# Gate logits by transposes and a VectorE sum instead of a product with a 0/1 matrix

## The chip, the cores and the metric

The kernel runs on one core of one Trainium2 chip. The metric is the device time of a run in microseconds (us); the median of three runs of the kernel before is 718.48 us (718.31 to 719.34). Engines are named as in the profile: PE is TensorE (PEld its weight loads), DVE is VectorE, ACT is ScalarE, POOL is GpSimd, SP is SyncE, which here only issues transfers.

## The reference

A linear attention with decay over 4 batches, 8 heads, 768 positions and 64 channels gives a matrix `x` of 3072 tokens by 512 columns. A mixture of 8 experts follows, in which every token goes to its two best experts. The change concerns the lines that compute `logits` and the argument of `noise_scale`, which are two products of `x` with 512 x 8 matrices.

```python
out[:, :, sl] = intra + inter                       # attention, block by block
kv_state = lam_block * kv_state + einsum('bhsd,bhse->bhde', kb_dec, vb)
...
x = attn_out.transpose(0, 2, 1, 3).reshape(B * S, H * D)     # 3072 x 512
...
logits = x @ w_gate                                 # 512 x 8
noise_scale = np.log1p(np.exp(x @ w_noise))         # 512 x 8
noisy_logits = logits + noise_scale * noise
top2 = np.argpartition(-noisy_logits, 2, axis=1)[:, :2]
...                                                 # softmax weights of the two
h = np.maximum(x[mask] @ w1[e], 0.0)
out[mask] += top2_w[mask, k, None] * (h @ w2[e])
```

## The kernel before

The attention handles 256 positions of all heads at once, as two chunks of 128, which is one unit `u` of 12. A loop over `t` from 0 to 11 (below: step 0 to step 11) is software-pipelined by hand: the order of the code is the order on every engine, since the schedule is manual. In step `t` the kernel does, in this order:

- `products(t-1)` and `turn_x(t-1)`: from the attention output `xo` of the unit before, four matmuls with the gate weights `wgn` (each leaves 32 rows of the PSUM tile `pR`, one for each of the four 128-column blocks of `x`, of which 16 are gate and noise products), copied by ACT into `xp` (128 rows x 2 chunks x 128 tokens); and eight transposes of `xo` into `xc`, which is stored to DRAM.
- `trans_k(t+1)`, `trans_q(t+1)`, `kv(t+1)`: transposes of keys and queries, scaling of the queries on DVE (`qTs`), and the decayed state `S`, which POOL multiplies and DVE adds to.
- `intra(t)`, `inter(t, 0)`, `evac_o(t)`: the output matmuls into `pO` and `pKV`.
- `logits(t-1)`: the rows of `xp` hold, for a token, four partial sums of each of 16 values, at rows 0, 32, 64 and 96 plus the value's number. Two matmuls (one for each chunk), with `xp` as the weights and the constant 0/1 matrix `sel` (128 x 16) as the moving operand, add the four and put tokens on the partitions, in the PSUM tile `pL`.
- `scores(t+1)`: 16 matmuls into four PSUM banks, which DVE multiplies with the decay mask into `at` (four instructions). The banks of `scores` are the ones that the transposes of the next step take, in the same order.

The PSUM tiles named `pS` rotate over four banks. `pL` is one bank; it holds the logits of a block in its first half and, in the second half, the counts and lists of the routing.

The routing works on blocks of 8 chunks (`GB`): block 0 is the chunks of units 0 to 3, and is worked on from step 4 on; block 1 from step 8 on; block 2 when the attention is over. It is a Python generator, `routing(b)`, that is drawn forward by `advance(n)` at three places of a step: in `kv` (by 4, `FILLC`), before `scores` (by 2, `FILLB`) and after them (by 18 to 24, `FILLA`). Each `yield` of the generator is one unit of `n`, mostly one small DVE instruction; `yield "step"` ends the `advance` that meets it, so that what follows begins at the next place. `gate(b)` begins with a copy of the block's logits from PSUM to `l2`. Then come `zc`, `ga`, an exponential (`gn` to `ge`), a logarithm (`glacc`), the noisy logits `nl`, the maxima `mx` and `mi`, the one-hot `oh` and `ob`; `weights(b)` (`wa` to `ws`, `recs`); `count(b)`, matmuls of `ob` on PE into `pL`; and `route(b)`: `own`, two large comparisons into a `wst` buffer (called `hot` in the code, five units each), `pos`, `past`, `rest`, then `yield "step"`, then 24 small matmuls (`tokab`) into `pL` with `hot` and `rest` as weights, and `whole`, `idx`, `found` and more on DVE.

POOL has, in steps 4 to 7, one `split_low` each (a subtraction over 128 x 1024 into `w1l`), which follows a one-element copy (`spacer`) that waits for `at`; in step 7 two gathers of token rows follow it, then the split of step 8 and the product for `S`.

After the loop, expert 0 begins on PE while DVE works on block 2. The setup of `sel` is seven DVE instructions in the prologue.

Of the kernel before, what the change touches and what calls it, by code (L numbers as in the profile page):

```python
# [21 lines left out]
FT = mybir.dt.float32  # L22
FR = mybir.dt.float32r
BF = mybir.dt.bfloat16
I32 = mybir.dt.int32
U32 = mybir.dt.uint32
AF = mybir.ActivationFunctionType
OP = mybir.AluOpType
AX = mybir.AxisListType

B, H, S, D = 4, 8, 768, 64
C = 128
# [4 lines left out]
DB = DM // 128  # L37
E = 8
# [32 lines left out]
GB = (0, 8, 16, NCH)  # L71
NG = len(GB) - 1
GM = max(GB[i + 1] - GB[i] for i in range(NG))
# [46 lines left out]
def kernel(  # L120
# [3 lines left out]
    nc = tc.nc  # L124
    MULT, ADD, SUB = OP.mult, OP.add, OP.subtract

    dram = ctx.enter_context(tc.tile_pool(name="dram", bufs=1, space=bass.MemoryType.DRAM))
    consts = ctx.enter_context(tc.tile_pool(name="consts", bufs=1))
    psum = ctx.enter_context(tc.tile_pool(name="psum", bufs=1, space=bass.MemoryType.PSUM))
    wp = ctx.enter_context(tc.tile_pool(name="wp", bufs=1, side="right"))  # L130
    rp = ctx.enter_context(tc.tile_pool(name="rp", bufs=1, side="right"))
    att = ExitStack()
    ac = att.enter_context(tc.tile_pool(name="ac", bufs=1))
    aw = att.enter_context(tc.tile_pool(name="aw", bufs=2))
# [39 lines left out]
    keep_warm(WARM[0])  # L174
    for nm in ("kt", "qt"):
        load(0, nm)
    jp = ac.tile([128, 128], I32, name="jp")
    nc.gpsimd.iota(jp, pattern=[[1, 128]], base=0, channel_multiplier=-1)
    identf = consts.tile([128, 128], FT, name="identf")
    nc.vector.tensor_scalar(identf, jp, 0.0, None, op0=OP.is_equal)  # L180
# [12 lines left out]
    p = psum.tile([128, H], FT, name="pL")  # L193
# [13 lines left out]
    p = psum.tile([128, HP, C], FT, name="pL")  # L207
# [1 line left out]
        nc.tensor.matmul(p[:, hp, :], hsel[:, hp].rearrange("h s i -> h (s i)"), pw[:, 127::-1], start=True, stop=True)  # L209
    nc.scalar.activation(QS, p, AF.Copy)  # L210
    nc.scalar.dma_start(mrev.rearrange("p i h -> p (i h)"), sub(powd, 0, [[H, 128], [1, C * H]]))

    sel = consts.tile([128, 2 * E], FT, name="sel")
    sq4 = ac.tile([128, 2 * E], FT, name="sq4")
    nc.vector.tensor_scalar(sel, jp[:, 0:2 * E], 0.0, None, op0=OP.is_equal)
    for d in range(1, DB):
        nc.vector.tensor_scalar(sq4, jp[:, 0:2 * E], float(-32 * d), None, op0=OP.is_equal)
        nc.vector.tensor_add(sel, sel, sq4)

    for nm in ("kt", "qt", "vt"):  # L220
        load(1, nm)
# [53 lines left out]
    jobs, scatters, PL = [], [], {}  # L275
# [23 lines left out]
    qT, qTs, kT, KD, AT, XO, XP, PO, SA, first = {}, {}, {}, {}, {}, {}, {}, {}, {}, {}  # L299

    pl, PC = None, {}
# [137 lines left out]

    def logits(u):  # L440
        nonlocal pl
        for a in range(2):
            g = 2 * u + a
            b = max(i for i in range(NG) if GB[i] <= g)
            if not g:
                pl = psum.tile([128, 512], FT, name="pL")
            if g == GB[b]:
                PL[b] = pl[:, b % 2 * 128:][:, :GM * 2 * E].rearrange("p (c e) -> p c e", e=2 * E)
                PC[b] = pl[:, 256 + b % 2 * 128:]
            nc.tensor.matmul(PL[b][:, g - GB[b], :], XP[u][:, a, :], sel, start=True, stop=True)  # L450


    def gate(b):
        v = nc.vector
        gs = GB[b + 1] - GB[b]
        sh = [128, gs, E]
        t = lambda sh, nm, dt=FT: rp.tile(sh, dt, name=nm)
        pl = PL[b]
        l2 = t([128, gs, 16], "l2")
        v.tensor_copy(l2, pl[:, :gs, :])  # L460
        yield
        zc = t(sh, "zc")
        v.tensor_scalar(zc, l2[:, :, 8:16], 87.0, -87.0, op0=OP.min, op1=OP.max)
        yield
        z = zc.rearrange("p c e -> p (c e)")
        fl = [128, gs * E]
        a = t(fl, "ga")
        v.scalar_tensor_tensor(a, z, -1.0, z, op0=MULT, op1=OP.max)
        yield
        e = t(fl, "ge")  # L470
        yield from exp_neg(nc, rp, e, a, fl, "g")
        acc = t(fl, "glacc")
        v.tensor_scalar(acc, e, LOGC[-1], None, op0=MULT)
        yield
        for c in LOGC[-2::-1]:
            v.scalar_tensor_tensor(acc, acc, c, e, op0=ADD, op1=MULT)
            yield
        acc3 = acc.rearrange("p (c e) -> p c e", e=E)
        v.scalar_tensor_tensor(acc3, l2[:, :, 8:16], 0.0, acc3, op0=OP.max, op1=ADD)
        yield  # L480
        nl = t(sh, "nl")
        v.tensor_mul(nl, acc.rearrange("p (c e) -> p c e", e=E), nz[:, GB[b]:GB[b + 1], :])
        yield
        v.tensor_add(nl, nl, l2[:, :, 0:8])
        yield
        mx = t(sh, "mx")
        mi = t(sh, "mi", U32)
        for c in range(gs):
            v.max(mx[:, c, :], nl[:, c, :])
            yield  # L490
        for c in range(gs):
            v.max_index(mi[:, c, :], mx[:, c, :], nl[:, c, :])
            yield
        ei = t([128, 2, gs], "ei")
        v.tensor_copy(ei.rearrange("p r c -> p c r"), mi[:, :, 0:2])
        yield
        oh = t([128, 2, gs, E], "oh")
        v.tensor_tensor(oh, iota8[:, :, :gs, :], ei[:, :, :, None].to_broadcast([128, 2, gs, E]), op=OP.is_equal)
        yield
        ob = t(sh, "ob", BF)  # L500
        v.tensor_add(ob, oh[:, 0], oh[:, 1])
        yield
        RT[b] = dict(mx=mx, ei=ei, oh=oh, ob=ob)
# [476 lines left out]
    for t in range(NST):  # L980
        u = t + 1
# [267 lines left out]
    with tc.For_i(0, n_over) as it:  # L1249
# [16 lines left out]
        for f in range(FB):  # L1266
            p = psum.tile([128, OV], FT, name="pS", bufs=4)
# [7 lines left out]
        p = psum.tile([OV, DM], FT, name="pO")  # L1275
# [35 lines left out]
```

## Time and profile before

| | |
|---|---|
| median of three runs | 718.48 us |
| the profiled execution, its own time | 711.21 us |
| its span, first to last instruction | 709.3 us |
| PE busy | 692.0 us (98%) |
| DVE, ACT, POOL busy | 358.1, 241.4, 287.3 us |
| granted TensorE clock, mean | 0.999 of full speed |
| `logits`, PE line L450 | 48 records for 24 matmuls, from 34.1 to 137.9 us |

The span is the profiled execution; about 1.9 us lie around it. Matmuls of 32-bit data show two records for each instruction, transposes one. A timeline row gives a start, the time from the start of the first to the end of the last of the instructions that it merges, the engine, the code line, the operation, the tiles (out<-in), the shape, the count and, in brackets, the idle time of the engine ahead of it with what ended it. A row of the chain of work gives a start, the time that the chain spent there, the engine, the tile and the line. A step of the attention takes about 10 us, and `pL L450` in a row marks its `logits`.

### The profile page before, as it was taken

How to read it: one execution, taken by the hardware profiler on the slowest of the kernel's cores; microseconds unless marked ns; L12 is line 12 of the kernel's file. 1: busy time of each engine (PE TensorE's matmuls, PEld its weight loads, DVE VectorE, ACT ScalarE, POOL GpSimd, SP SyncE). 2: the span in 40 equal slices, each digit the busy share in tenths (PEclk: the TensorE clock that was granted, in tenths of full speed). 3: DMA queues.
4: the chain of work that ended last, by engine and by line, in shares of the span. 5: the costliest groups of instructions: out<-in, count | busy, mean ns of one | idle time of the engine just before them, and what ended most of it. 6: DMA issues, size and time to landing. Idle time of an engine off the chain costs nothing.

```text
span 709.3 us, 13691 instructions
## 1 busy us (share of the span) xinstructions
PE 692.0 (98%) x5005; PEld 602.1 (85%) x5005; DVE 358.1 (50%) x817; ACT 241.4 (34%) x457; POOL 287.3 (41%) x447
## 2 busy tenths in 40 slices
PE   8899999899999999999999999999999999999996
PEld 6788888699898898889888988898988898889885
DVE  6345879787236565453635263635553454345211
ACT  1667785432133441231333133313422232304200
POOL 6211455677853547622144214424431524221311
PEclk9999999999999999999999999999999999999999
DMA  9999998582525668764377537756665646530211
GB/s 204 212 241 248 250 244 248 190 262 80 119 64 173 189 189 229 164 197 149 124 250 227 171 116 246 230 168 229 214 185 165 219 151 189 171 124 28 67 46 39
DMA packets 142731, 124.34 MB, mean 175 GB/s; under 512 B 88108, under 2 KB 110764, under 8 KB 142661
## 3 DMA queue, kind: packets, MB, share of 16 engines
q1 hardware_dynamic: 127844, 84.04, 44.2%
q0 software_dynamic: 14400, 38.87, 18.2%
q8 instruction: 40, 0.66, 0.4%
q10 hardware_dynamic: 416, 0.53, 0.2%
q14 instruction: 31, 0.25, 0.1%
HBM read 87.21 MB, written 37.32 MB: 176 GB/s over the span
## 4 chain that ended last, share of the span: by engine, by line
PE 75%; DVE 6%; DMA 6%; issue 6%; SPq 4%; ACT 1%; POOL 1%; POOLq 0%; DVEq 0%; ACTq 0%
PE pS L863 33%; PE pKV L906 12%; PE pO L906 12%; PE pS L932 4%; DMA turned<-ot 3%; PE pS L358 2%; PE pKV L371 2%; SPq L156 2%; PE pO L371 2%; SPq L842 1%; PE pS L431 1%; DMA crossed<-ot 1%; DVE at L361 1%; PE pS L315 1%; PE pS L328 1%
## 5 line engine op out<-in xcount | busy, mean ns | idle before, releaser
L863 PE MATMUL pS<-xth,w1h 128*128 128x512 f32 (+3 forms) x544 | 181.3, 333 | 2.0 <-DVE ht L873 1.6
L863 PE MATMUL pS<-xtl,w1h 128*128 128x512 f32 (+3 forms) x544 | 180.8, 332 | 0.5 <-DVE xtl L828 0.5
L863 PE MATMUL pS<-xth,w1l 128*128 128x512 f32 (+3 forms) x544 | 180.6, 332 | 0.0
L869 ACT ACTIVATE ht<-pS 128x512 fp32r<-128x512 f32 (+3 forms) x136 | 65.3, 482 | 220.8 <-PE pS L863 214.6
L873 DVE SCALAR_TENSOR_TENSOR ht<-pS,ht 128x256 fp32r<-128x256 f32 (+3 forms) x152 | 74.4, 501 | 104.8 <-ACT ht L869 102.8
L863 PEld LDWEIGHTS pS<-xth,w1h 128*128 128x128 f32 x544 | 102.8, 189 | 11.6 <-DVE ht L873 2.1
L863 PEld LDWEIGHTS pS<-xtl,w1h 128*128 128x128 f32 x544 | 102.8, 189 | 9.5 <-DVE xtl L828 0.6
L863 PEld LDWEIGHTS pS<-xth,w1l 128*128 128x128 f32 x544 | 102.8, 189 | 8.7
L906 PE MATMUL pKV<-w2h,ht 128*128 128x512 f32 x336 | 108.0, 393 | 0.0
L906 PE MATMUL pO<-w2h,ht 128*128 128x512 f32 x336 | 107.7, 392 | 0.0
L816 POOL DMA_INDIRECT xg<-x_tok,rec x46 | 52.7, 1145 | 90.4 <-DVE xtl L850 44.3
L906 PEld LDWEIGHTS pKV<-w2h,ht 128*128 128x128 f32 x336 | 63.2, 188 | 13.9
L906 PEld LDWEIGHTS pO<-w2h,ht 128*128 128x128 f32 x336 | 63.2, 188 | 13.7
L906 PE MATMUL pO<-w2l,ht 128*128 128x512 f32 x168 | 65.8, 391 | 0.0
L906 PE MATMUL pKV<-w2l,ht 128*128 128x512 f32 x168 | 65.8, 391 | 0.0
L960 POOL DMA_INDIRECT out_dram<-pv,rec x28 | 40.2, 1436 | 37.3 <-DVE pv L955 21.8
L625 POOL DMA_INDIRECT lst<-recs,dest x48 | 48.5, 1011 | 11.0 <-issue 8.3
L890 POOL DMA_INDIRECT pv<-out_dram,rec x39 | 40.0, 1027 | 28.5 <-issue 21.6
L960 POOL DMA_INDIRECT out_dram<-ot,rec x18 | 23.2, 1288 | 66.6 <-DVE ot L918 61.7
L849 ACT ACTIVATE xth<-xg 128x512 fp32r<-128x512 f32 (+1 forms) x39 | 22.7, 598 | 74.9 <-DMA xg<-turned 74.9
L1209 POOL COPY spacer<-ht 1x1 f32<-1x1 f32 x53 | 9.4, 177 | 88.0 <-ACT ht L869 87.9
L778 DVE TENSOR_TENSOR w2l<-wst,w2h 128x1024 fp32r<-128x1024 f32 (+1 forms) x33 | 38.1, 1155 | 9.4 <-ACT w2h L774 9.4
(240 smaller groups left out, 1030.0 us busy)
## 6 DMA issues: line engine op xcount, KB each, us to landing
wst<-in_moe_w_dram SPq DMA_DIRECT2D x48, 512.0 KB, 5.9
turned<-ot SPq DMA_DIRECT2D x36, 256.0 KB, 2.9
xg<-turned SPq DMA_DIRECT2D x144, 64.0 KB, 2.0
wst<-in_moe_w_dram SPq DMA_DIRECT2D x32, 256.0 KB, 4.1
kt<-in_k_dram SPq DMA_DIRECT2D x24, 256.0 KB, 5.9
qt<-in_q_dram SPq DMA_DIRECT2D x24, 256.0 KB, 6.7
vt<-in_v_dram SPq DMA_DIRECT2D x24, 256.0 KB, 5.6
x_tok<-xc POOLq DMA_DIRECT2D x8, 512.0 KB, 5.8
```

What stands on the lines that cost most here:

```text
L371: nc.tensor.matmul(PO[u][a][half(g), hp, :], lhs, rhs, start=n == 1, stop=n == (8 if u % NW or a else 4))
L625: st = nc.gpsimd.indirect_dma_start(out=lst, out_offset=bass.IndirectOffsetOnAxis(ap=r["dest"][:, i, c:c + 1], axis=0), in_=r["rec"][:, c, ...
L778: low.tensor_tensor(lo, st, hi.bitcast(FT), op=SUB)
L816: nc.gpsimd.indirect_dma_start(out=XG[t][:size(e, t)], out_offset=None, in_=x_tok[:rows, :], in_offset=bass.IndirectOffsetOnAxis(ap=at, ax ...
L849: nc.scalar.activation(hi, p, AF.Copy)
L863: nc.tensor.matmul(p, W1[a][d][:, fs], xt(b, cs)[:, d], start=(d == 0 and i == 0), stop=(d == DB - 1 and i == 2))
L869: nc.scalar.activation(ht(e, 0, f, cs), p, AF.Relu)
L873: nc.vector.scalar_tensor_tensor(ht(e, 1, f, c), p[:, r], 0.0, ht(e, 0, f, c).bitcast(FT), op0=OP.max, op1=SUB)
L890: nc.gpsimd.indirect_dma_start(out=PV[t][:size(e, t), :], out_offset=None, in_=out, in_offset=bass.IndirectOffsetOnAxis(ap=REC[e, t][:, 0: ...
L906: nc.tensor.matmul(p, ht(e, a, f, cs), W2[b][f // 2][:, f % 2, :], start=(i == 0), stop=(i == len(terms) - 1))
L932: nc.tensor.matmul(p, W2[b][f // 2][:, f % 2, d * 128:(d + 1) * 128], ht(e, a, f, cs), start=(i == 0), stop=(i == len(terms) - 1))
L960: st = nc.gpsimd.indirect_dma_start(out=out, out_offset=bass.IndirectOffsetOnAxis(ap=REC[e, t][:, 0:1], axis=0), in_=o, in_offset=None, bo ...
```

## The change

The two matmuls with `sel` become two transposes of `xp` with the identity `identf`, and one DVE reduction adds the four blocks, out of PSUM and into `l2` in SBUF, which is now allocated when a block's first logits come. So `gate` no longer begins with a copy, and its generator has one `yield` fewer. `sel` and its setup go. The integer matrix `jp` of the prologue takes a buffer of the tile `xc`.

```diff
-    jp = ac.tile([128, 128], I32, name="jp")
+    jp = aw.tile([128, 2, DB, C], FT, name="xc")[:, 0, 0, :].bitcast(I32)
...
-    sel = consts.tile([128, 2 * E], FT, name="sel")
-    sq4 = ac.tile([128, 2 * E], FT, name="sq4")
-    nc.vector.tensor_scalar(sel, jp[:, 0:2 * E], 0.0, None, op0=OP.is_equal)
-    for d in range(1, DB):
-        nc.vector.tensor_scalar(sq4, jp[:, 0:2 * E], float(-32 * d), None, op0=OP.is_equal)
-        nc.vector.tensor_add(sel, sel, sq4)
...
     def logits(u):
         nonlocal pl
+        g = 2 * u
+        b = max(i for i in range(NG) if GB[i] <= g)
+        if not g:
+            pl = psum.tile([128, 512], FT, name="pL")
+        if g == GB[b]:
+            PL[b] = (ac if b % 2 else rp).tile([128, GM, 2 * E], FT, name="l2")
+            PC[b] = pl[:, 256 + b % 2 * 128:]
+        p = pl[:, :2 * C].rearrange("p (a x) -> p a x", a=2)
         for a in range(2):
-            g = 2 * u + a
-            b = max(i for i in range(NG) if GB[i] <= g)
-            if not g:
-                pl = psum.tile([128, 512], FT, name="pL")
-            if g == GB[b]:
-                PL[b] = pl[:, b % 2 * 128:][:, :GM * 2 * E].rearrange("p (c e) -> p c e", e=2 * E)
-                PC[b] = pl[:, 256 + b % 2 * 128:]
-            nc.tensor.matmul(PL[b][:, g - GB[b], :], XP[u][:, a, :], sel, start=True, stop=True)
+            nc.tensor.transpose(p[:, a, :], XP[u][:, a, :], identf)
+        nc.vector.tensor_reduce(PL[b][:, g - GB[b]:g - GB[b] + 2, :],
+                                p.rearrange("p a (d e) -> p a e d", d=DB)[:, :, :2 * E, :], axis=AX.X, op=ADD)
...
     def gate(b):
-        pl = PL[b]
-        l2 = t([128, gs, 16], "l2")
-        v.tensor_copy(l2, pl[:, :gs, :])
-        yield
+        l2 = PL[b][:, :gs, :]
```

The generator is drawn by the same numbers, so each of its instructions now stands one place earlier. At most places that moves one small instruction across the four `at` of a step. In step 7 it moves more. On PE there, these are the rows of the program before from `logits` on (L450 is `logits`, L358 `scores`, L371 `inter`, L586 the small matmuls of `route(0)`).

```order
L450 MATMUL pL<-sel,xp 128x16 x2
L358 MATMUL pS<-qT,kT 128x128 x16
L371 MATMUL pKV<-qTs,S_171 64x128
L371 MATMUL pO<-qTs,S_170 64x128
L371 MATMUL pKV<-qTs,S_171 64x128
L371 MATMUL pO<-qTs,S_170 64x128
L371 MATMUL pKV<-qTs,S_171 64x128
L371 MATMUL pO<-qTs,S_170 64x128
L371 MATMUL pKV<-qTs,S_171 64x128
L371 MATMUL pO<-qTs,S_170 64x128
L586 LDWEIGHTS wst
L586 MATMUL pL<-tokab,wst 128x2
```

In the changed program (lines are 7 or 8 lower: L444 is the transposes, L578 the small matmuls) the same place of PE reads as follows.

```order
L364 MATMUL pKV<-qTs,S_160 64x128
L444 MATMUL pL<-identf,xp 128x128 x2
L578 LDWEIGHTS wst
L578 MATMUL pL<-tokab,wst 128x2
L578 LDWEIGHTS wst
```

And the end of the small matmuls in the changed program, on PE, with what follows them (L351 is `scores`).

```order
L578 LDWEIGHTS rest
L578 MATMUL pL<-tokab,rest 64x2
L351 MATMUL pS<-qT,kT 128x128 x16
L364 MATMUL pKV<-qTs,S_162 64x128
L364 MATMUL pO<-qTs,S_161 64x128
```

The 24 small matmuls of step 7 stood behind `scores` and `inter` and now stand ahead of them; since they write `pL`, the first of them also waits for the DVE reduction that reads `pL`. On DVE, before, step 7 from the query scaling on (L335 is `qTs`, L411 the state sum, L361 `at`):

```order
L335 TENSOR_TENSOR qTs<-pS,QS 128x4x128 x2
L411 TENSOR_TENSOR S_171<-S_171,pS 128x256
L571 SCALAR_TENSOR_TENSOR own<-ob,pos 128x8
L575 SCALAR_TENSOR_TENSOR rest<-own,last 128x512
L361 TENSOR_TENSOR at<-pS,Mk_130 128x512
L361 TENSOR_TENSOR at<-pS,Mk_131 128x512
L361 TENSOR_TENSOR at<-pS,Mk_130 128x512
L361 TENSOR_TENSOR at<-pS,Mk_131 128x512
L589 TENSOR_REDUCE whole<-pL 128x2
L591 CAST idx_186<-whole 128x2
L593 TENSOR_REDUCE found_190<-pL 64x1
```

The same stretch of DVE in the changed program (L445 is the new reduction, L354 `at`):

```order
L563 SCALAR_TENSOR_TENSOR own<-ob,pos 128x8
L328 TENSOR_TENSOR qTs<-pS,QS 128x4x128 x2
L404 TENSOR_TENSOR S_162<-S_162,pS 128x256
L567 SCALAR_TENSOR_TENSOR rest<-own,last 128x512
L445 TENSOR_REDUCE l_1240<-pL 128x32
L581 TENSOR_REDUCE whole<-pL 128x2
L583 CAST idx_177<-whole 128x2
L354 TENSOR_TENSOR at<-pS,Mk_130 128x512
L354 TENSOR_TENSOR at<-pS,Mk_131 128x512
L354 TENSOR_TENSOR at<-pS,Mk_130 128x512
L354 TENSOR_TENSOR at<-pS,Mk_131 128x512
L585 TENSOR_REDUCE found_181<-pL 64x1
```

`own` went ahead of `qTs`; the reduction, `whole` and `idx` now stand between `rest` and `at`. In step 10 the two large comparisons of block 1 stood together on DVE; in the changed program the reduction stands between them:

```order
L543 SCALAR_TENSOR_TENSOR own<-ob,pL 128x8
L547 SCALAR_TENSOR_TENSOR wst<-own,row 128x1024
L445 TENSOR_REDUCE l_2008<-pL 128x32
L547 SCALAR_TENSOR_TENSOR wst<-own,row 128x1024
L354 TENSOR_TENSOR at<-pS,Mk_130 128x512
```

The reduction there follows the transposes of the same step, which PE reaches behind `inter`. On ACT, POOL and SP no instruction moved.

## Rows read from the trace of the kernel before

**Rows 1.** The chain of work that ended last, steps 7 to 11.

```profile
94.05 0.55 PE pL L450 x4
...
97.18 0.83 PE pL L586 x24
...
106.47 2.46 DVE at L361 x4
...
122.63 0.23 DVE ob L501
...
125.95 0.55 PE pL L450 x4
...
131.85 0.59 PE pL L450 x4
```

**Rows 2.** Busy time by stretch: us, then PE, PEld, DVE, ACT, POOL.

```profile
core 0: us, PE busy (x) PEld busy (x) DVE busy (x) ACT busy (x) POOL busy (x), PEclk, DMA share, GB/s
...
84.00:94.00 10.00, 10.00 (x169) 8.69 (x165) 9.52 (x24) 7.34 (x18) 5.09 (x6) 1.00 1.12 261
...
114.00:124.00 10.00, 9.25 (x138) 7.64 (x138) 9.76 (x44) 5.45 (x12) 6.33 (x14) 1.00 0.99 293
```

**Rows 3.** Timeline of PE, step 4 (`logits`, `scores`) and step 5 (`turn_x`, `trans_k`).

```profile
64.29 0.62 PE L450 MATMUL pL<-sel,xp 128*128 128x16 f32 x4
64.84 2.06 PE L358 MATMUL pS<-qT,kT 64*128 64x128 f32 x32
...
67.99 1.09 PE L431 MATMUL pS<-identf,xo 128*128 128x128 f32 x8
68.92 1.04 PE L315 MATMUL pS<-identf,kt 128*128 128x128 f32 x8
```

**Rows 4.** Timeline of DVE: the two reductions nearest in size, and a large product out of PSUM.

```profile
98.12 0.15 DVE L589 TENSOR_REDUCE whole<-pL 128x2 f32<-128x4 f32 x1
...
99.37 0.29 DVE L606 TENSOR_REDUCE pp<-oh 128x16 f32<-128x128 f32 x1
...
102.28 0.69 DVE L335 TENSOR_TENSOR qTs<-pS,QS 128x512 f32<-128x512 f32 x1 [2.08 <-ACT qT L331]
```

**Rows 5.** Timeline of DVE, steps 5 to 7.

```profile
76.45 2.47 DVE L361 TENSOR_TENSOR at<-pS,Mk 128x512 f32<-128x512 f32 x4
...
85.80 2.48 DVE L361 TENSOR_TENSOR at<-pS,Mk 128x512 f32<-128x512 f32 x4 [0.20 <-PE pS L358]
88.20 0.98 DVE L521 TENSOR_SCALAR ws<-we 128x8 f32<-128x8 f32 x1
...
92.96 1.28 DVE L335 TENSOR_TENSOR qTs<-pS,QS 128x512 f32<-128x512 f32 x2
...
94.68 0.69 DVE L575 SCALAR_TENSOR_TENSOR rest<-own,last 128x512 bf16<-128x512 f32 x1
95.72 2.48 DVE L361 TENSOR_TENSOR at<-pS,Mk 128x512 f32<-128x512 f32 x4 [0.35 <-PE pS L358]
```

**Rows 6.** Timeline of POOL: the splits of steps 6 and 7, the state product of step 8.

```profile
86.77 2.38 POOL L778 TENSOR_TENSOR w1l<-wst,w1h 128x1024 fp32r<-128x1024 f32 x1
...
96.69 2.36 POOL L778 TENSOR_TENSOR w1l<-wst,w1h 128x1024 fp32r<-128x1024 f32 x1
...
104.19 0.62 POOL L410 TENSOR_TENSOR S<-S,QS 128x256 f32<-128x256 f32 x1
```

**Rows 7.** Timeline of DVE, step 8, and the two comparisons of step 10.

```profile
104.84 0.42 DVE L411 TENSOR_TENSOR S<-S,pR 128x256 f32<-128x256 f32 x1 [1.54 <-POOL S L410]
105.36 0.29 DVE L460 COPY l<-pL 128x128 f32<-128x128 f32 x1
...
106.44 2.48 DVE L361 TENSOR_TENSOR at<-pS,Mk 128x512 f32<-128x512 f32 x4 [0.56 <-PE pS L358]
...
124.49 2.36 DVE L555 SCALAR_TENSOR_TENSOR wst<-own,row 128x1024 bf16<-128x1024 f32 x2
```

**Rows 8.** Waits of PE from 134 to 240 us: total, times, longest.

```profile
PE pL L535 <- DVE ob L501: 0.2, 1, 0.2
```

## The prediction

> **What bounds the kernel now.** I read the busy shares first, then the chain of work that ended last, then the timelines of PE, DVE and POOL around the rows that the change touches. The shares say PE (98%), but `logits` occurs only in the attention, so that stage has to be read by itself. There the chain of work runs along PE from step 1 to step 8, and `logits` lies on it with 0.55 us each time, as in step 7 [rows 1]. From 106.47 us on it changes to DVE: through `at` of step 8 and the gate of block 1 as far as `ob` at 122.63. PE then waits for `ob`; the rest of the way is mixed: `logits` of step 10 (125.95), `at`, the routing, `logits` of step 11 (131.85), expert 0. The busy times agree: from 84 to 94 us PE is full and DVE has 0.48 us left; from 114 to 124 us DVE is full and PE is not [rows 2]. So PE time is worth something up to step 8 only if DVE, which has almost nothing to spare from step 5 on, can follow. After 160 us PE is the bound and any shift passes through unchanged.
>
> **What goes, and its price.** *PE.* `logits` takes 64.84 - 64.29 = 0.55 us to the next group's start [rows 3]. Eight transposes of the same kind (32-bit, 128 x 128, the same identity) take 68.92 - 67.99 = 0.93 us [rows 3], so two take 0.23. The saving is 0.32 us a step; its bounds are 0 (the transposes take the old slot of 0.55 after all) and 0.32. *DVE.* The reduction reads 128 elements a partition out of PSUM and writes 32. The nearest rows are the sum over 128 elements (0.29 us) and the sum over 4 (0.15) on one side, and a product of 512 elements out of PSUM (0.69) on the other [rows 4]. I take 0.27 from one start to the next, as the 0.29 row is the nearest; the bounds are 0.15 and 0.69. There are twelve of them. Three copies of 0.29 go [rows 7], and so do seven setup instructions in the prologue: these are hidden by DVE's idle time ahead of the first key copy, which waits for PE and its first keys, and I count nothing for them.
>
> [...]
>
> **Steps 1 to 6.** In steps 1 to 4 DVE waits for PE, and the reduction fits in that wait: it needs the transposes alone, while `at` needs the first half of `scores`, which comes 95.72 - 94.60 = 1.12 us after `scores` begin (94.05 + 0.55 = 94.60 [rows 1], [rows 5]). So `at` of step 4 begins 4 x 0.32 = 1.3 us earlier. In step 5 `at` followed its predecessor on DVE with no idle time (76.45), in step 6 with 0.20 [rows 5]. There DVE sets the pace: two reductions cost 0.54. PE meets this in step 6, where its transposes want the banks that `at` of step 5 frees: I count a stall of 0.2 us. PE then comes to `logits` of step 7 6 x 0.32 - 0.2 = 1.7 us early, at 92.35, and is done with it at 92.6.
>
> **Step 7.** Here the moved order decides. The 24 small matmuls now stand ahead of `scores`, and the first of them waits for the reduction, which stands behind `rest` on DVE. When is `rest` done? Before, at 95.72 - 0.35 = 95.37 [rows 5]. Now: minus 1.3 (step 4), plus 0.54 (two reductions), minus the 0.20 that was idle, minus some 0.45 because the list stands one place further ahead. That last term is worth more than one small instruction: `ws` took 0.98 us, and ended at 89.18, when POOL's split, begun at 86.77, ended (89.15) [rows 5, 6]; it now goes ahead of `at`, and only what follows the split's end counts. The sum is -1.4: `rest` ends at 94.0, the reduction at 94.25. PE has waited 1.65 us for it, nearly all that it had gained. The small matmuls take 0.83 [rows 1]; `scores` begin at 95.08 instead of 94.60, and `at` at 96.2 instead of 95.72. Since the 0.83 no longer follows `inter`, what comes after on PE is 0.83 - 0.48 = 0.35 us earlier than before. If the split delays nothing, `rest` ends 0.7 earlier, and so does all this.
>
> **Step 8.** PE would let `at` begin 0.35 + 0.32 = 0.67 earlier. But POOL's split of step 7 waits for `at` of step 7 (+0.48); two gathers, the next split and the state product follow it in POOL's order, the last at 104.19 [rows 6], and DVE's state sum, before at 104.84 after a wait of 1.54 for that product [rows 7], waits for it. It moves to 105.32. Behind it come the reduction in the place of the copy, `zc`, and now `ga` too: before, the copy and `zc` were done at 106.44 - 0.56 = 105.88 [rows 7]; now 105.88 + 0.48, less 0.02, and `ga` makes 106.5 or a little less. `at` of step 8 begins where it was (106.44), at best 0.7 earlier. So the gain of PE's eight `logits` has gone almost entirely: to DVE, to the moved small matmuls, and to POOL behind them.
>
> **Steps 9 to 11 and expert 0.** From `at` of step 8 to `ob` DVE does the same work, with one more reduction (0.27) and one small instruction less on either side: about 0. In step 10 the reduction stands between two comparisons of 2.36 / 2 = 1.18 us each and waits for PE's transposes: the first comparison ends at 125.67 [rows 7], the transposes begin at 125.95 [rows 1] and give their result at about 126.25. DVE idles 0.6, and `at` begins at 126.5 + 1.18 = 127.7; before it was 126.50 + 1.12 = 127.62. So +0.1, and the saving of that `logits` is lost too. In step 11 `logits` is on the chain of work, after a wait for DVE: -0.3 remains. In expert 0 block 2 has no copy any more, and PE's one wait of 0.2 us for its `ob` [rows 8] goes: -0.2.
>
> The sum is 0 + 0.1 - 0.3 - 0.2 = -0.4 with the split's hold as I read it, and -1.1 without. I take -0.7, nearer to the first. The profiled execution (711.21, of which the span is 709.3) would become 710.5. It is 7.3 us below the median of the runs; the difference carries over, and the prediction is 718.48 - 0.7 = 717.8 us.
>
> **The rivals.** *The saving goes through.* PE keeps 0.32 in eight steps, and the two last terms: -2.6 - 0.5 = -3.1, 715.4. For it: `logits` is on the chain eight times in a row. Against it: `rest` was done only 0.35 us before `at` had to begin, and POOL's wait in step 8.
>
> *The reduction is dear, and the kernel slower.* At 0.69 it costs 0.42 more each time. It counts in six steps: 5 and 6 (ahead of `rest`), 7 (ahead of the small matmuls), 8, 9 and 10. That is 6 x 0.42 = 2.5, less 0.7: +1.8, 720.3. It decides from 0.12 more on, a reduction of about 0.4 us, and is measurable from 0.63. For it: the reduction's operand is read with a stride, which no row here does out of PSUM. Against it: 0.29 for as many elements with a stride of one.
>
> *The transposes save nothing*, because weight loads or the start of a group set the 0.55: then PE gains nothing, the small matmuls of step 7 come when `rest` is done at 95.4 or later, and POOL's chain moves with them: +0.5 to +1, about 719.2. Against it: the same transposes cost 0.116 each in their groups.
>
> **How the numbers follow.** Below about 0.2% (1.4 us) a difference can't be told from none here. Chances: the likeliest, 0.62, with a range of its own of 717.0 to 718.4; the saving goes through, 0.18; the dear reduction, 0.13; no saving, 0.07. Faster by over 0.2% (below 717.04) takes in the second and a tenth of the first: 0.24. Slower (above 719.92) is two thirds of the third and a little of the last: 0.10. The same: 0.66. The range is 716.0 to 719.8: it leaves out most of the second case and half of the third.
>
> **What would show it.** Right: two transposes in about 0.23 us on PE; reductions of about 0.29; in step 7 PE idle by over 1 us ahead of the small matmuls, with DVE's reduction as releaser; `at` of step 8 behind a wait for POOL; in step 10 an idle DVE ahead of the reduction. Wrong: if `scores` of step 7 begin before 94 us the stall is smaller than I make it, most of the 2.6 us is kept, and the time is near 715.5; if reductions take 0.5 or more, the kernel is slower. A change outside the attention (tiles of the later stage laid out anew, other waits there) is not in the sum at all.

## The result, and the profile after

The changed kernel is slower: 727.12 us (median of 6 runs, 724.50 to 728.49) against 717.86 us of the kernel before (6 runs beside it), a ratio of 1.0131 with an interval of 1.0111 to 1.0150. The prediction was 717.8 us, no change. Its profiled execution took 727.13 us, of which the span is 725.3, at a mean granted clock of 0.986.

Inside the attention the trace shows the new instructions much as they were priced. First the groups of the two new lines (duration min, median, max in ns; first and last start).

```profile
L444 PE MATMUL pL<-identf,xp x24: 272/314/421, 34.9 to 142.2; 128*128 128x128 f32 x24
```

```profile
L445 DVE TENSOR_REDUCE l<-pL x12: 281/289/293, 35.4 to 143.5; 128x32 f32<-128x128 f32 x12
its engine sat idle before it (us, times) until:
  PE pL L444: 4.8, 6
who waited for it (us, times):
  PE pL L578: 1.3, 1
```

PE waited for a reduction once, 1.3 us. That is step 7, in the timeline of PE:

```profile
93.84 0.44 PE L444 MATMUL pL<-identf,xp 128*128 128x128 f32 x2
95.55 0.54 PE L578 MATMUL pL<-tokab,wst 128*128 128x2 bf16 x16 [1.28 <-DVE l L445]
96.02 0.41 PE L578 MATMUL pL<-tokab,rest 128*64 128x2 bf16 x8
96.36 3.21 PE L351 MATMUL pS<-qT,kT 64*128 64x128 f32 x32
```

PE sits idle for 1.28 us ahead of the small matmuls, as forecast in kind (1.65). What was not forecast is the last row: `scores` takes 3.21 us, where the same matmuls took 2.06 in step 4 of before [rows 3]. The table of stretches says why: the column in front of the last two is the granted clock.

```profile
core 0: us, PE busy (x) PEld busy (x) DVE busy (x) ACT busy (x) POOL busy (x), PEclk, DMA share, GB/s
...
84.00:94.00 10.00, 10.00 (x167) 8.51 (x164) 9.69 (x27) 7.39 (x18) 5.16 (x6) 1.00 1.14 269
...
97.00:100.00 3.00, 3.00 (x36) 2.78 (x36) 1.69 (x3) 1.37 (x3) 1.27 (x2) 0.50 1.10 225
...
114.00:124.00 10.00, 9.94 (x150) 7.95 (x147) 9.55 (x48) 6.52 (x17) 4.19 (x10) 1.00 0.54 154
...
134.00:144.00 10.00, 6.29 (x71) 4.64 (x72) 5.70 (x26) 2.66 (x5) 6.41 (x16) 0.87 0.98 298
144.00:154.00 10.00, 10.00 (x86) 9.92 (x86) 2.54 (x9) 3.38 (x8) 2.65 (x5) 0.79 0.51 176
```

From 97 to 100 us, behind the idle stretch, the granted clock was 0.50. From 84 to 94 us PE is full as before; from 114 to 124 us PE is now full (9.94) and DVE is not (9.55), where before it was the other way round [rows 2]. `at` of step 8 came 2.42 us late (the last row here against 106.44 in [rows 7]). Not all of that is from step 7: `scores` of step 1 had begun 0.64 us late (35.29 against 34.65), behind an earlier stretch at a low granted clock (0.50 from 22 to 24 us).

```profile
107.10 0.42 DVE L404 TENSOR_TENSOR S<-S,pR 128x256 f32<-128x256 f32 x1 [0.73 <-POOL S L403]
107.78 0.29 DVE L445 TENSOR_REDUCE l<-pL 128x32 f32<-128x128 f32 x1 [0.26 <-PE pL L444]
...
108.86 1.29 DVE L354 TENSOR_TENSOR at<-pS,Mk 128x512 f32<-128x512 f32 x2 [0.30 <-PE pS L351]
```

The larger loss lies behind the attention, where the diff changes no line. The chain of work there, then the timeline of ACT:

```profile
148.19 0.61 ACT xc L425
148.81 2.91 DMA x_tok<-xc
151.82 0.39 ACT ht L861
```

```profile
139.07 0.60 ACT L384 ACTIVATE xo<-pO 128x512 f32<-128x512 f32 x1 [5.46 <-remote]
...
148.19 0.60 ACT L425 ACTIVATE xc<-pS 128x512 f32<-128x512 f32 x1 [0.37 <-PE pS L424]
151.82 0.66 ACT L861 ACTIVATE ht<-pS 128x256 fp32r<-128x256 f32 x2 [3.04 <-DMA x_tok<-xc]
```

In the kernel before, `ht` followed `xc` at once:

```profile
141.48 1.09 ACT L432 ACTIVATE xc<-pS 128x512 f32<-128x512 f32 x2 [2.95 <-PE pS L431]
142.45 0.39 ACT L869 ACTIVATE ht<-pS 128x256 fp32r<-128x256 f32 x1
```

Expert 0's first `ht` now waits for the store of the last unit's `xc` to DRAM, which it has nothing to do with. ACT's 5.46 us ahead of `xo` are of this execution alone: in the second profile of the same kernel (group 2) ACT waits 3.82 us there, for PE, as before (3.69), and the wait of `ht` is there again:

```profile
148.63 0.66 ACT L861 ACTIVATE ht<-pS 128x256 fp32r<-128x256 f32 x2 [4.69 <-DMA x_tok<-xc]
```

The program's allocation tells what ties the two: in the kernel before `ht` has bytes 22176 to 75424 of each partition and the two `xc` buffers lie from 98368 on; in the changed kernel `ht` begins at 22112, and `xc` lies at 52160 to 60352, inside it. The diff does that: `jp` is now taken out of the first `xc` tile, so that `xc` is placed early in its pool, and the dropped `sel` (64 bytes a partition) let everything behind it slide.

### The profile page after: what moved, and what is told of

Its sections match the earlier page's. It is cut to its first block, busy times and chain, and to the rows that moved or that the text cites. A ratio compares the mean times of both kernels' runs of the same rounds, so it can differ in the third digit from the quotient of the medians.

```text
span 725.3 us, 13649 instructions
## 1 busy us (share of the span) xinstructions
PE 699.7 (96%) x4981; PEld 602.2 (83%) x4981; DVE 358.6 (49%) x819; ACT 241.9 (33%) x457; POOL 287.8 (40%) x447
## 4 chain that ended last, share of the span: by engine, by line
PE 77%; DVE 8%; issue 6%; DMA 3%; SPq 2%; POOL 2%; another core or an unknown queue 1%; ACT 1%; POOLq 0%; ACTq 0%
PE pS L855 35%; PE pKV L898 13%; PE pO L898 12%; PE pS L924 5%; PE pS L351 2%; SPq L156 2%; DVE at L354 2%; PE pKV L364 2%; PE pO L364 1%; PE pS L817 1%; PE pS L424 1%; DMA vt<-in_v_dram 1%; POOL out_dram L952 1%; DVE glacc L468 1%
## 5 line engine op out<-in xcount | busy, mean ns | idle before, releaser
L898 PE MATMUL pKV<-w2h,ht 128*128 128x512 f32 x336 | 109.7, 398 | 0.0
L808 POOL DMA_INDIRECT xg<-x_tok,rec x46 | 50.8, 1104 | 84.2 <-DMA rec<-lst 33.4
L952 POOL DMA_INDIRECT out_dram<-pv,rec x28 | 42.3, 1512 | 37.9 <-DVE pv L947 20.7
```

Source lines behind the costliest of these rows:

```text
L808: nc.gpsimd.indirect_dma_start(out=XG[t][:size(e, t)], out_offset=None, in_=x_tok[:rows, :], in_offset=bass.IndirectOffsetOnAxis(ap=at, ax ...
L898: nc.tensor.matmul(p, ht(e, a, f, cs), W2[b][f // 2][:, f % 2, :], start=(i == 0), stop=(i == len(terms) - 1))
L952: st = nc.gpsimd.indirect_dma_start(out=out, out_offset=bass.IndirectOffsetOnAxis(ap=REC[e, t][:, 0:1], axis=0), in_=o, in_offset=None, bo ...
```

## The experiments

All ratios are to the kernel before in the same group of runs. The groups ran on several chips, on which the kernel before took from 709.9 to 717.6 us, so times in us are not compared across groups, and the first four expectations, written in us against 717.9 and 727.1, are to be read as ratios (720 to 722 is 1.003 to 1.006, 722 to 725 is 1.006 to 1.010, 724 to 725 is 1.0085 to 1.010, 717 to 718.5 is 0.999 to 1.001).

**Group 1: undoing the side effects.** The first run moves `jp` out of `xc`:

```diff
-    jp = aw.tile([128, 2, DB, C], FT, name="xc")[:, 0, 0, :].bitcast(I32)
+    jp = wp.tile([128, F], FT, name="wst", bufs=4)[:, :128].bitcast(I32)
```

> The changed kernel, with the index matrix jp in a tile of the weight staging ring instead of in the first xc tile, so that xc lies behind qTs and xp again as in the kernel before, and no longer under the ht tile of expert 0. Theory of the layout: expert 0's first ht no longer waits for the last store of x_tok (151.82 us in the changed kernel, 142.45 before); it begins near 145, and the time falls from 727.1 by 5 to 7 us to 720 to 722, with the 2.4 us of step 7 left. Rival (the transposes and the reduction cost the time themselves, by DVE time or by a lower clock of TensorE): the first ht is late anyway and the time stays within 1.5 us of 727.

The second makes the opposite edit alone in the kernel before:

```diff
-    jp = ac.tile([128, 128], I32, name="jp")
+    jp = aw.tile([128, 2, DB, C], FT, name="xc")[:, 0, 0, :].bitcast(I32)
```

> The kernel before, with one edit: jp in the first xc tile, so that xc comes to lie under the ht tile of expert 0. The products with the 0/1 matrix and the order of the work are as before. Theory of the layout: the first ht of expert 0 waits for the last store of x_tok and begins some 5 us late (near 148 instead of 142.45); the time is 722 to 725 instead of 717.9. Rival (transposes and reduction): no change, 717 to 719.

The third restores the order, by one `yield` in the changed kernel; the fourth has this and the edit of the first.

```diff
         l2 = PL[b][:, :gs, :]
+        yield
```

> The changed kernel with one more yield at the start of the gate, so that the routing of a block advances as it did before, and the 24 small matmuls of step 7 stand behind scores again. Layout as in the changed kernel. Theory of the moved order: no idle PE ahead of the small matmuls of step 7, no stretch at a granted clock of 0.50 in 97 to 100 us, at of step 8 near 106 instead of 108.88; the time falls by 2 to 3 us to 724 to 725, if the wait of the first ht doesn't take it back (it hangs on the last store of x, which moves along). Rival (the idle stretch comes from the reduction itself, or from the transposes): time and step 7 stay as they are, 727.

> The changed kernel with jp in the staging ring and with the additional yield: only the transposes and the reductions in place of the products are left of the change. If layout and moved order are the whole loss, 717 to 718.5, the time of the kernel before within 0.2%. If the transposes and the reduction cost time themselves, 720 or more. If their saving goes through, 715 to 716.5.

Measured: layout undone 1.0052 (1.0033 to 1.0070), layout alone 1.0045 (1.0028 to 1.0061), order undone 1.0076 (1.0057 to 1.0096), both undone 1.0029 (1.0018 to 1.0040). The first is as expected, the second and the third are somewhat lower. The two answers on the place of `xc` agree: 0.45% alone, and 0.76 - 0.29 = 0.47% between the third and the fourth. The timeline of ACT in the run with the layout alone has the wait, with products, `sel` and order as before:

```profile
141.31 1.09 ACT L432 ACTIVATE xc<-pS 128x512 f32<-128x512 f32 x2 [2.94 <-PE pS L431]
147.14 0.66 ACT L869 ACTIVATE ht<-pS 128x256 fp32r<-128x256 f32 x2 [4.75 <-DMA x_tok<-xc]
```

The price of the moved order is 0.52 - 0.29 = 0.23% here. But the fourth run doesn't fit: with both undone 0.29% is left, although its trace was 1 us ahead of before at `scores` of step 7 (93.38 us against 94.53, by the timelines). Something later took 3 us.

**Group 2: the rest.** The changed kernel again; the rest with `jp` in the free `l2` tile and the order undone; and two single edits in the kernel before (`jp` in the staging ring; no `yield` behind the gate's copy).

```diff
+    jp = ac.tile([128, GM, 2 * E], FT, name="l2").rearrange("p c e -> p (c e)").bitcast(I32)
```

> The changed kernel as it is, beside the three runs that follow. From the four runs so far (layout 0.45 to 0.47%, moved order 0.23%, rest 0.29% of the kernel before): if the parts add up and nothing else is in it, the ratio is 1.0099, with the first ht of expert 0 at about 148 us and scores of step 7 at about 95.5 with a granted clock of 1.00 behind them. If the fall of the granted clock to 0.50 behind the idle stretch of step 7 belongs to the change (rival: it belongs to the executions in which it was seen), the ratio is 1.013 again and the clock of 97 to 100 us is near 0.5.

> The changed kernel with jp in the l2 tile of block 1 (which is free at that time), and with the additional yield: xc lies behind qTs and xp, the order is that of before, and the ring of the weight staging is not touched, other than in the run with both undone, which measured 1.0029. If the transposes and the reduction themselves cost those 2 us, 1.003 again. If the shifted staging ring cost them, 0.998 to 1.000.

> The kernel before with one edit, jp as the first tile of the weight staging ring, so that every later tile of that ring moves on by one slot. If the ring is what the run with both undone lost, 1.002 to 1.004; if transposes and reduction lost it, 0.999 to 1.001.

> The kernel before with one edit, no yield behind the copy of the gate's logits, so that the routing runs one instruction ahead and the 24 small matmuls of step 7 stand ahead of scores. No transposes, no reduction, no new layout. Theory of the moved order: PE idles ahead of the small matmuls until rest is done, scores of step 7 begin near 95.5 instead of 94.5, at of step 8 follows, and the ratio is 1.001 to 1.0025. Rival: without the reduction, rest is done when PE arrives, nothing waits, and the ratio is 1.000.

Measured: 1.0150 (1.0130 to 1.0170); 1.0019 (1.0000 to 1.0038); 1.0003 (0.9986 to 1.0020); 0.9992 (0.9976 to 1.0009). The changed kernel loses as much on another chip, and again with a granted clock of 0.64 (94 to 97 us) behind the idle stretch of step 7 (`scores` 3.44 us long). So the parts of group 1 don't add up to it: they make 0.47 + 0.23 + 0.29 = 0.99%. The longer `scores` (1.4 us, 0.2%) cover less than half of the difference; the rest of it stays open. The ring costs nothing.

The order alone costs nothing that the runs can tell, so the expectation of 1.001 to 1.0025 was wrong in the time: without the reduction PE waits only 0.35 us for `rest`. Its trace has `scores` of step 7 late as expected (95.78), but `at` of step 8 only 0.5 us late (106.97 against 106.45), less than these runs resolve. With transposes and reductions the same order costs 1.6 us at `at` of step 8 (106.73 in the first run of group 1, 105.12 in the fourth). Whether that is because the reduction stands between `rest` and the small matmuls, or because PE has gained some 1 us by then and loses it, no run separates.

What the rest loses showed in the last expert's gemm2, in matmuls with `ht` as moving operand. The first and the last of 48 `w2l` matmuls (every third of the stretch) in the run with the ring, where `ht` begins at 22176:

```profile
668.67 0.39 PE L906 MATMUL pO<-w2l,ht 128*128 128x512 f32 x1
...
700.94 0.39 PE L906 MATMUL pKV<-w2l,ht 128*128 128x512 f32 x1
```

That is 32.27 us. In all six traces at hand with `ht` at 22112 it is 32.76 or 32.77, at a granted clock of 1.00 and with PE busy throughout. PE executes the same instructions there; only the place of `ht`, and the number of PE instructions ahead, differ.

**Group 3: the place of `ht`.** An unused constant moves `ht` and what follows (64 or 32 bytes); and the kernel before with `sel` in another pool has `ht` at 22112, with every instruction kept. In that run all tiles behind `sel` move by the same 64 bytes, not `ht` alone, but the tiles of keys, queries and values, `xc`, and the expert's weights stay.

```diff
+    pad = consts.tile([128, 16], FT, name="pad")
+    nc.vector.memset(pad, 0.0)
```

```diff
-    sel = consts.tile([128, 2 * E], FT, name="sel")
+    sel = ac.tile([128, 2 * E], FT, name="sel")
```

> The run of the rest of the change (jp in l2, order undone) plus one unused constant of 64 bytes a partition, which takes the place of the dropped matrix sel: ht begins at byte 22176 of a partition again, as in the kernel before, instead of 22112. In the runs so far the matmuls of gemm2 follow each other in 0.2322 us wherever ht begins at 22112 and in 0.2286 us wherever it begins at 22176 (48 triples of the last expert: 32.77 against 32.27 us). If the place of ht sets that pace, gemm2 is back at 32.27, some 3 us come back and the ratio is 0.996 to 0.999. Rival (PE's instruction stream, which is 24 instructions shorter, sets it): 32.77 and 1.002 to 1.003 again.

> The same with a constant of 32 bytes: ht begins at 22144, a multiple of 128 bytes. If the place of ht sets the pace of gemm2 and a multiple of 128 is its best, 32.3 us or less for the 48 triples (0.2275 us a matmul, the pace of gemm1, would make 32.1) and a ratio of 0.995 to 0.998. If every place other than 22176 is bad: 32.77 and 1.002. Rival (instruction stream): 32.77.

> The kernel before with one edit: sel in the pool of the attention's constants instead of the pool of the constants, so that ht begins at 22112 as in the changed kernel. All instructions and their order as before, xc not under ht. If the place of ht sets the pace of gemm2: 32.77 us for the 48 triples and a ratio of 1.004 to 1.005. Rival (instruction stream): 32.27 and 1.000.

> The changed kernel with the unused constant of 64 bytes, so that of its three side effects only two are left (xc under ht, the moved order). If the place of ht is worth what the gemm2 rows say (3.2 us): 1.009 to 1.011 instead of 1.015. Rival (instruction stream): 1.015.

Measured: 0.9968 (0.9937 to 0.9998) with 32.27 us; 1.0050 (1.0023 to 1.0077) with 32.90; 1.0067 (1.0041 to 1.0093) with 32.77; 1.0056 (1.0031 to 1.0080) with 32.27. So it is the place, and for gemm2 the place of `ht`, the only operand of these matmuls in SBUF that moves: the kernel before, with one small tile in another pool and no other edit, loses 0.67%. Its rows:

```profile
680.94 0.40 PE L906 MATMUL pO<-w2l,ht 128*128 128x512 f32 x1
...
713.71 0.39 PE L906 MATMUL pKV<-w2l,ht 128*128 128x512 f32 x1
```

The stretches of gemm2 behind 250 us give a lower figure: four of them took 33.12 or 33.13 us before and 33.62 to 33.64 with `ht` at 22112, three 22.14 and 22.45, in sum 4 x 0.50 + 3 x 0.31 = 2.9 us or 0.41%, which is the lower end of the interval. What the rest of the 0.67% is, or whether it is noise, is not shown. The guess on multiples of 128 bytes was wrong, since 22144 is the worst place so far. And the last run gained more than expected (1.0056 instead of 1.009 to 1.011); the place of the key tiles, which the next groups come to, is the likely reason.

**Group 4: what is left, and two more places.**

> The changed kernel with jp in the l2 tile and the unused constant of 64 bytes: both changes of the layout are undone (xc not under ht, ht at 22176), while the transposes, the reductions and the moved order stay. This is what the prediction costed. If its sum is right (the stall of step 7 takes back what logits gain), the ratio is 0.999 to 1.001 and at of step 8 begins within 0.5 us of before. If the moved order costs more than that by a lower clock behind the idle stretch of step 7 (granted clock of 94 to 104 us at 0.83), 1.002 to 1.004. If it costs nothing, the ratio is that of the next run.

> The kernel of the 64 byte constant with the order undone as well, beside the run above on one chip: only transposes and reductions are left of the change. 0.996 to 0.9985 if the 0.9968 of the other chip holds. The difference to the run above is the price of the moved order: 1 to 2 us by the prediction's steps, 0 if the idle stretch of step 7 is hidden.

> The same with 96 bytes: ht at 22208, 64 bytes past a multiple of 128. So far 22112 (96 past) gave 32.77 us for the 48 triples of gemm2, 22144 (0 past) 32.90, 22176 (32 past) 32.27. If the distance to a multiple of 128 sets the pace, a fourth value or one of the three comes out, and the time follows at 8 times the difference; if only the distance of 64 bytes to some multiple mattered (22144 and 22208 alike), 32.90.

> The same with 128 bytes: ht at 22240, which is 128 bytes behind 22112. If the pace of gemm2 goes by the distance to a multiple of 128 bytes, 32.77 us again and a ratio of 1.001 to 1.003; if it goes by a larger unit or by the place itself, something else.

Measured: 0.9997 (0.9976 to 1.0017); 0.9962 (0.9940 to 0.9983); 1.0043 (1.0027 to 1.0060) with 32.90 us; 0.9962 (0.9941 to 0.9983) with 31.96. Over the five places 22112, 22144, 22176, 22208 and 22240 gemm2 took 32.77, 32.90, 32.27, 32.90 and 31.96 us. 22112 and 22240 are 128 bytes apart and differ by 0.81, so the distance to a multiple of 128 doesn't set it. What unit does stays open. The price of the moved order is 0.9997 - 0.9962 = 0.35% in this group. In the trace of the first of these runs the clock falls again behind step 7's idle stretch, which ends at 91.39 us there:

```profile
94.00:97.00 3.00, 3.00 (x37) 1.85 (x34) 2.54 (x7) 0.21 (x1) 2.58 (x3) 0.57 1.07 243
```

The traces with 64 bytes of padding show one more thing, far ahead of `ht`. In step 0 (the expectations of group 5 call it step 1) ACT scales the keys of a later unit (`kd`) and waits for their load. These are its rows in the kernel before, then in the second run of this group:

```profile
23.75 2.45 ACT L343 ACTIVATE kd<-kt,pwt 128x128 f32<-128x128 f32 x8 [3.89 <-DMA kt<-in_k_dram]
```

```profile
21.31 2.45 ACT L338 ACTIVATE kd<-kt,pwt 128x128 f32<-128x128 f32 x8 [2.16 <-DMA kt<-in_k_dram]
```

With 64 bytes in the one pool `kt`, `qt` and `vt`, into which keys, queries and values are loaded, stand at multiples of 512 bytes (35840 and so on); in none of the others so far. `kd` begins at 20.42 to 22.27 us in the four traces that have them there, and at 23.26 to 23.94 in all that have them elsewhere (in six of these the wait ends with a matmul of PE, not with the load). The transfers run better there, too: from 2 to 26 us the DMA engines moved 227 to 246 GB/s in the four, at a DMA share of 0.97 to 1.08, and 214 to 222 GB/s at 1.11 to 1.20 in the others. So the 0.9997 of the first run of this group, which looks like the prediction come true, has this gain in it.

**Group 5: places held fixed, and the best places.** The first run has 64 bytes of padding in each of two pools, so that `ht`, `xc`, `kt`, `qt` and `vt` stand where the kernel before has them (a few constants of the attention, the decay masks and `QS` among them, stand 64 bytes further). The second has the order undone, the 64 bytes, and one small tile moved between the pools.

```diff
+    pad2 = ac.tile([128, 16], FT, name="pad2")
+    nc.vector.memset(pad2, 0.0)
```

```diff
-    pwt = ac.tile([128, 2, H], FT, name="pwt")
+    pwt = consts.tile([128, 2, H], FT, name="pwt")
```

> The changed kernel with jp in the l2 tile and an unused constant of 64 bytes in each of two pools, so that every tile of the attention and ht stand at the bytes of the kernel before (kt 35904, xc 98368, ht 22176); the order stays moved. It is what the prediction costed, and nothing else. By the prediction's sum 0.999 (its range of the likeliest case 0.998 to 1.000). If the clock that falls behind the idle stretch of step 7 costs what it did in the changed kernel's own profiles (scores 1.2 to 1.4 us longer): 1.001 to 1.003. If the earlier runs with kt at 35840 owe part of their time to that place (kt a multiple of 512 there; scores of step 1 began at 21.6 to 23.4 us instead of 24.2), this run is slower than the 0.9997 of the run with 64 bytes in one pool, by up to 2.4 us.

> Transposes and reductions, order undone, with jp in l2, 64 bytes of unused constant and one small tile (64 bytes) moved from the attention's constants to the constants: ht at 22240 (31.96 us for the 48 triples of gemm2, the best of five places) and kt at 35840 (a multiple of 512). If the two gains of place are real and add up: 0.992 to 0.9945, scores of step 1 before 23.5 us, 31.96 us for the triples. If the early start of the runs with kt at 35840 had another cause: 0.996, scores of step 1 near 24.2.

Measured: 1.0025 (1.0000 to 1.0050), and 0.9929 (0.9897 to 0.9961), which is some 5 us faster than the kernel before. The second bears out both gains of place: gemm2 took 31.96 us and `kd` began early.

```profile
21.22 2.45 ACT L338 ACTIVATE kd<-kt,pwt 128x128 f32<-128x128 f32 x8 [0.57 <-DMA kt<-in_k_dram]
```

That is some 2 us ahead of the 23.26 to 23.94 us at the other places. What unit of bytes counts for the place of these tiles is not shown.

The first, with the timeline of PE and then of DVE, is the test of the prediction's own steps:

```profile
94.21 0.54 PE L582 MATMUL pL<-tokab,wst 128*128 128x2 bf16 x16 [1.26 <-DVE l L449]
94.68 0.41 PE L582 MATMUL pL<-tokab,rest 128*64 128x2 bf16 x8
95.02 2.06 PE L355 MATMUL pS<-qT,kT 64*128 64x128 f32 x32
```

```profile
96.21 2.48 DVE L358 TENSOR_TENSOR at<-pS,Mk 128x512 f32<-128x512 f32 x4 [0.72 <-PE pS L355]
...
105.19 0.42 DVE L408 TENSOR_TENSOR S<-S,pR 128x256 f32<-128x256 f32 x1 [2.08 <-POOL S L407]
...
106.26 1.89 DVE L358 TENSOR_TENSOR at<-pS,Mk 128x512 f32<-128x512 f32 x3
...
126.27 0.29 DVE L449 TENSOR_REDUCE l<-pL 128x32 f32<-128x128 f32 x1 [0.64 <-PE pL L448]
126.48 1.22 DVE L551 SCALAR_TENSOR_TENSOR wst<-own,row 128x1024 bf16<-128x1024 f32 x1
127.61 2.48 DVE L358 TENSOR_TENSOR at<-pS,Mk 128x512 f32<-128x512 f32 x4
```

In this execution the same idle stretch of 1.26 us was not followed by a lower clock in step 7, but the clock was at 0.75 later:

```profile
97.00:100.00 3.00, 3.00 (x43) 2.41 (x42) 2.97 (x6) 1.56 (x5) 2.79 (x3) 1.00 1.18 229
...
134.00:144.00 10.00, 6.74 (x53) 5.24 (x50) 4.34 (x15) 2.67 (x5) 6.41 (x14) 0.75 0.83 262
```

The later fall need not be the work of step 7's idle stretch: the run with `sel` moved alone (group 3), which has neither the reductions nor the moved order, shows it too.

```profile
134.00:144.00 10.00, 7.22 (x58) 6.00 (x53) 4.08 (x13) 2.66 (x5) 6.49 (x14) 0.71 0.82 267
```

The 12 runs of the kernel with its places fixed had a mean granted clock of 0.990 (median), the 20 of the kernel before 0.9935. By a line through the times of both kernels over their clocks, a run is 0.34 us longer for each 0.001 less, and at one clock the two kernels are level, give or take 1.2 us. So the 1.8 us go with the clock here. That the change lowers the clock is not shown: the first run of group 4, with the same order and reductions, had the median clock of the kernel before beside it (0.992).

## Why the prediction was wrong

**The failed step is the last sentence of the prediction**: "A change outside the attention (tiles of the later stage laid out anew, other waits there) is not in the sum at all." What it left out was four fifths of the result (0.67 + 0.45 of 1.37), or three quarters, if the place of `ht` is taken by the rows of gemm2 alone (0.41 + 0.45 of 1.11). That the tiles move, and that `ht` then has to wait for the store of `xc`, follows from the diff and the allocation; what the place of `ht` costs no row of before could show.

| part | shown by | of the time |
|---|---|---|
| place of `ht` (22176 to 22112) | `sel` moved alone | +0.67% (0.41 to 0.93) |
| `xc` under `ht` | `jp` moved alone | +0.45% (0.28 to 0.61) |
| transposes, reductions, order, main places fixed | padding in two pools | +0.25% (0.00 to 0.50) |
| sum, over two chips | | +1.37% (0.97 to 1.77) |
| the change itself | two groups of runs | +1.31% and +1.50% |

*Transposes.* The saving was mis-sized: not 0.32 but 0.18 us a step. Two transposes stand 0.37 us apart from the next group and not 0.23, against 0.55 [rows 3]. The rows are of the run with both undone (group 1), PE and then DVE:

```profile
93.01 0.44 PE L444 MATMUL pL<-identf,xp 128*128 128x128 f32 x2
93.38 2.06 PE L351 MATMUL pS<-qT,kT 64*128 64x128 f32 x32
```

```profile
94.58 0.28 DVE L445 TENSOR_REDUCE l<-pL 128x32 f32<-128x128 f32 x1
94.78 2.47 DVE L354 TENSOR_TENSOR at<-pS,Mk 128x512 f32<-128x512 f32 x4
```

The price taken was that of eight in a row; why two alone are dearer was not tried.

*Reductions.* They were cheaper than priced. The price of 0.27 was from one start to the next, and by that they take 0.20 us where the next instruction doesn't need the sum (94.58 to 94.78). Each lasts 0.289 us (median), as its nearest row did (0.29), but that is another measure. The rival of the dear reduction is out.

*Step 7.* Right in kind and nearly in size, with the main places fixed: `scores` at 95.02 (forecast 95.08), `at` at 96.21 (96.2), PE idle for 1.26 (1.65). The gain ahead of it was smaller than forecast (1.1 us, not 1.7, from `scores` of step 0 on), and that execution had begun these `scores` 0.4 us early (23.88 against 24.27), so that a part of this closeness is luck. What the step left out is the clock: in three of six traces with this idle stretch (both of the changed kernel, and the first of group 4) it fell behind it (to 0.50 from 97 to 100 us, and to 0.64 and 0.57 from 94 to 97), at a price of 0.9 to 1.4 us in `scores` alone (2.91 to 3.44 instead of 2.06).

*Step 8 and 10.* Right: DVE's state sum waits for POOL at 105.19 (105.32), `at` begins at 106.26 (106.44). In step 10 DVE idled 0.64 us ahead of the reduction (0.6), and `at` began at 127.61 (127.7). The two gains forecast behind it (0.3 and 0.2 us) can't be read in this trace, as the granted clock is lower there (0.75 from 134 to 144 us).

*The rival "the saving goes through"* is what the kernel does when the order is undone: at `at` of step 8 the clean run of group 2 stood at 105.18, 1.29 us ahead of the run with the ring alone (106.47, same group). With the moved order that is gone, as predicted: the 0.23 to 0.35% that undoing it gave in whole runs (1.7 to 2.5 us) is of that size. The rival that transposes save nothing is out.

So the mechanism inside the attention was read rightly, apart from the clock. With the main places fixed it came to +0.25% (0.00 to 0.50), and to nothing, give or take 1.2 us, at one clock; the forecast was -0.7 us. The sum was wrong by what it excluded.

## What to carry to other kernels

Before costing an edit, compare the allocation of the two programs: a tile borrowed for a moment can fix the place of a whole ring, and the next stage then waits for a transfer that it never needed; a few bytes dropped from a pool of constants shift every tile behind. Measure an edit with all places held fixed by padding, and try other places too: here they moved the transposes and reductions, with the order undone, from 1.0050 to 0.9929 of the kernel before. The kernel before with the best places was not run, so how much of these 5 us is owed to the places alone is not shown. Where an instruction is put between two others that PE waits for, price the clock behind the idle stretch too, not only the stretch: where it fell here, `scores` took 2.91 to 3.44 us instead of 2.06.

## What the runs showed of the hardware

The pace of matmuls with a moving operand of 128 x 512 32-bit values went with the place in the partition where that operand begins: 0.229 us a matmul with `ht` at 22176 (32.27 / 47 / 3) and 0.232 at 22112 (32.77 / 47 / 3), both at a granted clock of 1.00; over the five places it was 0.227 at best (31.96 / 47 / 3) and 0.233 at worst (32.90 / 47 / 3). The good places found (22176, 22240) and the bad ones (22112, 22144, 22208) follow no rule that five places could show. With the tiles of keys, queries and values at multiples of 512 bytes the DMA engines moved 227 to 246 GB/s instead of 214 to 222 from 2 to 26 us, and the scaling of the keys, which waits for them, began at 20.4 to 22.3 us instead of 23.3 to 23.9. And an idle stretch of PE of 1.28 us in step 7 was followed by a granted clock of 0.50 (97 to 100 us) in the changed kernel's first profile, while one of 1.26 us, of the same cause and in the same place, was followed by 1.00 (94 to 104 us) in the run with the places held fixed; what decides between them is open, as is ACT's wait of 5.46 us ("remote") in step 11 of the changed kernel's first profile, which its second doesn't show.
